# Regrouping the products with v and moving the row sums, transposes and cluster chain of a fused attention and expert kernel

## The chip, the cores and the metric

One core of a Trainium2 chip runs the whole program. The metric is device time in microseconds (us) for one execution, the median of several. Five engines work side by side and wait for each other by semaphores: PE (TensorE, matrix products), DVE (VectorE), ACT (ScalarE), POOL (GpSimd) and SP, which here issues DMAs. Each engine runs its instructions in the order in which they were written.

## The reference

Clustered attention for 4 batches of 8 heads, 768 tokens and head size 64, followed by a routed expert layer.

```python
def _attn_ref(q, k, v, centroids):
    ...
    q_assign = np.argmax(np.einsum('bhsd,hcd->bhsc', q_n, c_n), axis=-1)
    k_assign = np.argmax(np.einsum('bhsd,hcd->bhsc', k_n, c_n), axis=-1)
    mask = q_assign[:, :, :, None] == k_assign[:, :, None, :]
    scores = scale * np.matmul(q, k.transpose(0, 1, 3, 2))
    scores = np.where(mask, scores, -1000000000.0)
    scores = scores - np.max(scores, axis=-1, keepdims=True)
    attn = np.exp(scores)
    attn = attn / (np.sum(attn, axis=-1, keepdims=True) + 1e-09)
    return np.matmul(attn, v).astype(np.float32)
```

Then `_moe_ref` adds to each token whose `x @ w_skip` is positive the gated output of one of eight two-layer experts (512 to 1024 to 512), chosen by argmax.

## The kernel before

Two heads form a pair, and 16 pairs run one after the other (some 440 us); the experts follow (some 200 us) and are not touched. A pair has 24 steps, one per score tile: two query halves `hf` of 384 columns, six key tiles `kt` of 128, two heads `a`, so step s = 12 hf + 2 kt + a. `steps` fills a heap of tasks with times in units of one step, counted from the pair's step 0, and pops them in order of time: the tables PLAN, FIRST, GATES and SLOTS are these times. So they fix the order in which every engine's instructions are written; they are no times on the chip. A function that yields a number goes on that much later; one that yields a tuple goes on at that time of its own pair.

What recurs in each pair, with its lines:

- `score` (L631, L632): two products into one PSUM bank, exp by ACT into one of 12 PT buffers (L634), and a running sum over keys `acc` by POOL (L640, L646).
- `smax` (L582, L584), one per step, for the next pair: a product into a bank and a DVE maximum over it. `mneg` (L598), `mrows` (L606, L617) turn the maxima into rows of the next operands.
- `avs` (L657): the products of PT with v, two heads side by side in 64 columns each, accumulated over key tiles in bank 7. One call does GROUP = 3 key tiles, so there are four calls in a pair; ACT then moves the result to `oT`.
- `sims` (L488) and the chain `assign` / `first_max` (L521 to L528) on DVE give each token's cluster, two pairs ahead; `masks` (L545), `split_hi` (L429, ACT) and `split_lo` (L439, DVE) prepare operands.
- `sums` (L693), `recip` (L705, L710), `xout` (L756 transposes; L778 scaling by ACT, or L761 by DVE in the last three pairs) finish the pair before and store it.
- Once per batch (four pairs) the routing runs over three pairs: `logits_in`, then `route_gates` (L843, L847) with `choose` (L901 to L919) and `gate` (L928 to L945), then `route_c` (L955 to L981), `route_d` (L991 rhs, L996 product) and `route_e`.

PSUM has eight banks. `take` gives out seven of them first in, first out, and `give` puts one back; bank 7 belongs to `avs`. An engine that writes a bank again waits until the reader of its last contents is done.

Products of `score` and `smax` use the array as one block of 128 columns, `avs` as two of 64, `sims`, `sums` and `logits_in` as four of 32.

Of the kernel before, what the change touches and what calls it, by code (L numbers as in the profile page):

```python
# [13 lines left out]
F32 = mybir.dt.float32  # L14
# [4 lines left out]
AF = mybir.ActivationFunctionType  # L19
ALU = mybir.AluOpType  # L20
# [25 lines left out]


PLAN = {
    "load": -60.0, "load_v": -45.0, "weights": 72.0, "sims": -42.9, "assign": (-42.45, 0.07, 0.02, 2.0, 0.02, 0.02),
    "hi": (-40.35, -34.25), "masks": (-34.5, 0.12), "lo": (-34.35, -28.35), "copies": (-23.3, -23.2, -23.1),  # L50
    "smax": (-21.1, 1.0, -0.4), "mneg": (-9.0, 3.2), "mrows": ((-4.5, 0.2, 0.05), (5.5, 0.1, 0.05)),
    "av": 1.6, "oT": (3.5, 3.55), "sums": 29.2, "recip": 31.5, "xout": (31.52, 49.55, 37.55),
    "route": (29.25, 34.9, 58.9), "early": (85.4, 100.9),
}

GATES = (35.0, 35.4, 37.66, 43.67, 43.68, 49.66, 49.67, 49.68, 49.69, 49.7, 49.71, 50.5,
         53.16, 53.17, 53.18, 61.67, 61.68, 67.67, 67.68, 73.66, 73.67)
SLOTS = (59.1, 59.11, 59.12, 59.13, 73.7, 73.71, 77.16, 77.17, 77.18, 77.19, 79.66, 82.9, 83.1,
         91.67, 91.68, 97.66, 97.67, 97.68, 97.69, 97.7)
CODES = {91.67: 85.9, 91.68: 85.91}  # L60
FIRST = {
    0: {
        "load_v": -18.9, "sims": -20.0, "hi": (-19.9, -19.8, -19.7, -19.6), "assign": (-19.0, 0.1, 0.01, 0.01, 0.01, 0.01),
        "lo": (-18.7, -18.6, -16.9, -16.8), "masks": -17.0, "smax": (-14.0, 0.1, 14.1, 0.55), "mneg": (-12.85, 7.55),
        "mrows": ((-12.8, 0.1, 0.0), (8.2, 0.1, 0.0)),
    },
    1: {
        "sims": -42.2, "hi": (-42.4, -42.3), "lo": (-40.1, -40.0), "copies": (-20.9, -20.8, -20.7), "load_v": -14.0,
        "assign": (-36.83, 12.93, 0.2, 0.2, 0.2, 0.2), "masks": (-21.6, 0.1), "smax": (-16.3, 0.95, -0.1),
        "mneg": (-5.3, 5.9), "mrows": ((-4.3, 0.2, 0.05), (6.4, 0.1, 0.05)),  # L70
    },
    2: {
        "load": -62.0, "load_v": -37.0, "hi": (-34.25, -28.3), "lo": (-28.35, -22.35), "copies": (-23.3, -23.2, -22.2),
        "assign": (-34.6, 0.25, 0.02, 6.0, 0.02, 0.02), "masks": (-26.0, 0.12), "smax": (-17.6, 0.97, 0.0), "mneg": (-6.4, 5.2),
    },
    3: {"assign": (-41.95, 0.07, 0.02, 1.5, 0.02, 0.02)},
}

GROUP = 3


class Kernel:
# [242 lines left out]

    def tasks(self, i):

        p, last = {**PLAN, **FIRST.get(i, {})}, i == self.npair - 1
# [319 lines left out]
    def avs(self, i, hf, kts):  # L648
        c, nc = self.st[i], self.nc
        if kts[0] == 0:  # L650
            c["av"] = self.banks[7][:, :HALF + 1]
        av = c["av"]
        first = None
        for kt in kts:
# [9 lines left out]
        if kts[-1] == KT - 1:
            p = PLAN["oT"]
            if hf == 0:
                c["oT"] = self.OT[i % 5]
            last, oT = i == self.npair - 1, c["oT"][:, hf * HALF:(hf + 1) * HALF]
            if not last or hf == 0:
                yield 0.05 if last else 1.0  # L670
            vm = self.small.tile([P, 1], F32, name="vm")
            if last and hf == 0:
                nc.vector.tensor_copy(vm, av[:, HALF:])
                nc.vector.tensor_scalar(out=oT, in0=av[:, :HALF], scalar1=vm, scalar2=None, op0=ALU.add)
                return
            if not last and hf:
                nc.scalar.activation(out=vm, in_=av[:, HALF:], func=AF.Copy)
                yield p[hf] - 1.0
                nc.scalar.activation(out=oT, in_=av[:, :HALF], func=AF.Identity, bias=vm)
            else:  # L680
                if not last:
                    yield p[hf] - 1.0
                nc.scalar.activation(out=vm, in_=av[:, HALF:], func=AF.Copy)
                nc.scalar.activation(out=oT, in_=av[:, :HALF], func=AF.Identity, bias=vm)
# [459 lines left out]
    def ending(self, i):  # L1144
# [15 lines left out]
        for t, c, k in ((25.8, 0, 0), (25.87, 0, 1), (25.94, 0, 2), (25.95, 0, 3), (25.96, 1, 0), (26.05, 1, 1),  # L1160
# [363 lines left out]
```

## Time and profile before

| | us |
|---|---|
| median of 3 runs | 643.86 (643.77 to 643.98) |
| profiled execution, its own time | 643.63 |
| its span, first to last instruction | 641.9 |
| PE busy | 621.7 (97%) |
| DVE busy | 506.0 (79%) |
| ACT busy | 425.9 (66%) |
| POOL busy | 364.0 (57%) |

In the attention stage POOL's share is far above its mean: it is idle in the experts' stage. The granted clock of PE is the full one all the way (0.997 on average). A PE row's duration runs to the modelled end of a pipelined product; what a product costs PE is the step from its start to the next one's start.

### The profile page before, as it was taken

To read this page: it belongs to the slowest core of one execution; us is meant where nothing else is said; L and a number is where in the kernel's file an instruction comes from. 1 tells how busy PE (TensorE), PEld (TensorE's weight loads), DVE (VectorE), ACT (ScalarE), POOL (GpSimd) and SP (SyncE) were. 2 spreads that over 40 slices of the span, in tenths; PEclk is the share of its full clock that TensorE was granted. 3 is DMA by queue.
4 is the path that set the end of the run, shared out by engine and by line. 5 is a ranking of instruction groups with operands and counts; after the bars stand their busy time and mean duration, and the time that the engine had idled before them with its cause. 6 is when DMAs were issued, how large, how long until landed. Compare 5 with 4: busy or idle time off the path is not lost.

```text
span 641.9 us, 12202 instructions
## 1 busy us (share of the span) xinstructions
PE 621.7 (97%) x3873; PEld 459.2 (72%) x3873; DVE 506.0 (79%) x1047; ACT 425.9 (66%) x963; POOL 364.0 (57%) x384
## 2 busy tenths in 40 slices
PE   7899999999999999999999999999999999999994
PEld 3566776676667766666767676646799899899793
DVE  6898787699998869999879997885889765855721
ACT  7377788788778877877878878833644644645510
POOL 8697887867867967778777778522043212121101
PEclk9999999999999999999999999999999999999998
DMA  7397748866786466555754652332395766765610
GB/s 215 92 228 204 189 125 210 228 205 176 206 231 179 129 172 168 170 140 162 206 151 124 174 135 75 99 117 86 117 312 196 255 222 223 240 206 177 240 44 36
DMA packets 54322, 110.10 MB, mean 172 GB/s; under 512 B 8599, under 2 KB 22807, under 8 KB 54256
## 3 DMA queue, kind: packets, MB, share of 16 engines
q1 hardware_dynamic: 51232, 101.92, 54.7%
q0 software_dynamic: 2624, 7.18, 3.3%
q8 instruction: 32, 0.52, 0.3%
q14 instruction: 34, 0.28, 0.2%
q10 hardware_dynamic: 400, 0.20, 0.1%
HBM read 60.93 MB, written 10.55 MB: 111 GB/s over the span
## 4 chain that ended last, share of the span: by engine, by line
PE 72%; DMA 10%; issue 9%; DVE 7%; ACT 1%; POOL 0%; POOLq 0%; DVEq 0%; ACTq 0%
PE ps L657 20%; PE ps L631 11%; PE ps L582 11%; PE ps L632 10%; DMA out<-yo,idw 7%; DMA xg<-out,idr 2%; PE ps L488 2%; DVE M L584 2%; PE ph L1058 2%; PE ph L1057 2%; PE ph L1056 2%; PE ps L693 2%; PE ps L756 2%; PE py L1057 1%; PE py L1056 1%
## 5 line engine op out<-in xcount | busy, mean ns | idle before, releaser
L646 POOL TENSOR_TENSOR acc<-acc,PT 128x384 f32<-128x384 f32 x246 | 244.0, 1020 | 42.2 <-ACT PT L634 41.9
L634 ACT ACTIVATE PT<-ps 128x384 f32<-128x384 f32 x384 | 183.2, 492 | 74.2 <-PE ps L632 62.1
L584 DVE TENSOR_REDUCE M<-ps 128x1 f32<-128x384 f32 x384 | 198.5, 550 | 40.3 <-PE ps L582 40.0
L657 PE MATMUL ps<-PT,vt 128*64 128x385 f32 x768 | 138.4, 495 | 0.1
L631 PE MATMUL ps<-D 102*128 102x384 f32 x384 | 134.9, 351 | 2.3 <-DVE M L584 1.7
L582 PE MATMUL ps<-D 96*128 96x384 f32 x384 | 134.4, 356 | 1.0 <-ACT D L562 1.0
L632 PE MATMUL ps<-D 128*128 128x384 f32 x384 | 130.0, 339 | 0.0
L657 PEld LDWEIGHTS ps<-PT,vt 128*64 128x64 f32 x768 | 49.3, 136 | 59.9 <-issue 55.3
L631 PEld LDWEIGHTS ps<-D 102*128 102x128 f32 x384 | 72.8, 190 | 23.8 <-issue 18.6
L582 PEld LDWEIGHTS ps<-D 96*128 96x128 f32 x384 | 73.5, 192 | 21.0 <-issue 14.4
L640 POOL TENSOR_TENSOR acc<-PT 128x384 f32<-128x384 f32 x64 | 54.5, 870 | 58.4 <-ACT PT L634 37.1
L1214 POOL DMA_INDIRECT out<-yo,idw x15 | 20.0, 1335 | 112.6 <-DVE yo L1090 95.3
L632 PEld LDWEIGHTS ps<-D 128*128 128x128 f32 x384 | 73.0, 190 | 0.0
L1342 ACT ACTIVATE hh<-ph 128x256 fp32r<-128x256 f32 x56 | 21.4, 383 | 46.4 <-PE ph L1058 46.4
L1343 DVE SCALAR_TENSOR_TENSOR hl<-ph,hh 128x256 fp32r<-128x256 f32 x56 | 23.6, 422 | 33.6 <-ACT hh L1342 33.6
L1314 ACT ACTIVATE D<-wraw 128x1024 fp32r<-128x1024 f32 (+1 forms) x45 | 44.2, 1002 | 6.5 <-PE py L1058 4.7
L1056 PE MATMUL ph<-x2l,D 128*128 128x256 f32 x168 | 47.7, 284 | 0.0
L1057 PE MATMUL ph<-x2h,D 128*128 128x256 f32 x168 | 47.5, 283 | 0.0
L1056 PE MATMUL py<-D,hh 128*128 128x512 f32 x112 | 45.0, 402 | 0.0
L1315 DVE TENSOR_TENSOR D<-wraw,D 128x1024 fp32r<-128x1024 f32 (+1 forms) x29 | 34.3, 1183 | 6.3 <-ACT D L1314 5.6
L778 ACT ACTIVATE x<-ps,rs 128x64 f32<-128x64 f32 x162 | 36.1, 322 | 3.5 <-issue 1.2
L439 DVE TENSOR_TENSOR raw<-raw,D 128x768 fp32r<-128x768 f32 x28 | 38.2, 1363 | 0.0
(314 smaller groups left out, 1050.5 us busy)
## 6 DMA issues: line engine op xcount, KB each, us to landing
wraw<-w SPq DMA_DIRECT2D x72, 512.0 KB, 4.7
D<-D SPq DMA_DIRECT2D x124, 192.0 KB, 3.4
raw<-qk SPq DMA_DIRECT2D x16, 768.0 KB, 5.5
D<-raw SPq DMA_DIRECT2D x60, 192.0 KB, 4.2
vt<-v SPq DMA_DIRECT2D x16, 384.0 KB, 4.6
out<-x SPq DMA_DIRECT2D x31, 192.0 KB, 3.6
D<-mk SPq DMA_DIRECT2D x120, 24.0 KB, 2.0
out<-yo,idw POOLq DMA_INDIRECT x15, 4.3
```

Source lines behind the costliest of these rows:

```text
L439: eng.tensor_tensor(out=lo.bitcast(F32R), in0=lo, in1=c[f"hi{t}"].bitcast(F32), op=ALU.subtract)
L582: nc.tensor.matmul(sm, lhsT=c["qm"][a][0:96, j * P:(j + 1) * P], rhs=c["kb"][a][0:96, hf * HALF:(hf + 1) * HALF], start=True, stop=True)
L584: nc.vector.tensor_reduce(out=c["m"][:, j, a, hf:hf + 1], in_=sm, axis=AX.X, op=ALU.max)
L631: nc.tensor.matmul(ps, lhsT=c["kb"][a][:MR, ks], rhs=c["qm"][a][:MR, sl], start=True, stop=False)
L632: nc.tensor.matmul(ps, lhsT=c["kc"][a][:, ks], rhs=c["qc"][a][:, sl], start=False, stop=True)
L634: nc.scalar.activation(out=pt, in_=ps, func=AF.Exp, scale=D ** -0.5)
L640: nc.gpsimd.tensor_tensor(out=acc, in0=self.pt(i, s - 2)[:, :HALF], in1=pt, op=ALU.add)
L646: (nc.vector if dve else nc.gpsimd).tensor_tensor(out=acc, in0=acc, in1=pt, op=ALU.add)
L657: nc.tensor.matmul(av[a * D:(a + 1) * D, :], lhsT=c["vt"][:, kt, a * D:(a + 1) * D], rhs=self.pt(i, hf * 2 * KT + kt * 2 + a), start=(kt = ...
L1056: mm(ps, lhsT=ah, rhs=bl, start=first, stop=False)
L1057: mm(ps, lhsT=ah, rhs=bh, start=False, stop=False)
L1314: nc.scalar.activation(out=h[:, cs], in_=r[:, cs], func=AF.Copy)
```

## The change

A call of `avs` now takes four key tiles, and its tiles may lie in both query halves: three calls in a pair (two halves' key tiles 0 to 3; 4, 5 and 0, 1; 2 to 5). The last pair keeps groups of three. Each half has a bank of its own from the rotation, which now has eight banks, and `av_out` gives it back. `sums`, `recip`, the transposes of `xout`, and `mrows` stand next to a group of `avs`. `sims` and `sums` stand in front of different groups. `assign` is cut in two: the maximum, the comparison and the multiplication beside one group, the rest beside the next. Both `split_lo` of a pair, and most of the routing's DVE work, stand directly behind each other after a group. `xout` of the first half is scaled by DVE in every pair.

```diff
-    "av": 1.6, "oT": (3.5, 3.55), "sums": 29.2, "recip": 31.5, "xout": (31.52, 49.55, 37.55),
+    "av": 1.6, "oT": (0.35, 3.55), "sums": 33.06, "recip": 33.64, "xout": (33.66, 49.55, 41.55),
...
-GROUP = 3
+GROUP = (4, 3)
...
         self.free = deque(range(7))
+        self.spare = [7]
...
-            for g in range(0, KT, GROUP):
-                add(12 * hf + 2 * (g + GROUP) + p["av"], self.avs, hf, range(g, g + GROUP))
+        n = GROUP[last]
+        keys = [(hf, kt) for hf in range(2) for kt in range(KT)]
+        for g in range(n, 2 * KT + 1, n):
+            add(2 * g + p["av"], self.avs, keys[g - n:g])
...
-        b = self.held[key] = self.free.popleft()
+        b = self.held[key] = self.spare.pop() if key == ("av", 0) and self.spare else self.free.popleft()
...
+        mark, first = c["exp%d%d" % keys[-1]], True
+        for hf, kt in keys:
+            if kt == 0:
+                c["av", hf] = self.take(("av", hf), [P, HALF + 1])
+            av = c["av", hf]
             for a in range(2):
...
+            nc.scalar.activation(out=vm, in_=av[:, HALF:], func=AF.Copy)
...
+            nc.scalar.activation(out=oT, in_=av[:, :HALF], func=AF.Identity, bias=vm)
+            if last:
                 self.out_mark = self.newest()
+        self.give(("av", hf))
...
-        if i >= self.npair - 3:
+        if i >= self.npair - 3 or hf == 0:
             self.scale_out(i, hf, xp)
```

The first place is PE's order in a pair in the middle, around the products of `sims` (raw, cb) and `sums` (acc, ones); L582 and L586 are `smax`, L631/L632 and L635/L636 `score`, L606 and L610 `mrows`, L657 and L661 `avs`. Before:

```order
L488 MATMUL ps_85<-raw,cb_175 32x384 x2
L488 MATMUL ps_85<-raw,cb_179 32x384 x2
L693 MATMUL ps_82<-acc,ones 32x384 x4
L606 MATMUL ps_87<-ident,MX_190 128x128
L582 MATMUL ps_84<-D 128x384
```

Now, from the end of one stretch of scores:

```order
L492 MATMUL ps_81<-raw,cb_175 32x384 x2
L492 MATMUL ps_81<-raw,cb_179 32x384 x2
L586 MATMUL ps_88<-D 128x384
L764 MATMUL ps_83<-ident,oT_97 128x128 x3
L661 MATMUL ps_87<-PT,vt 64x385 x8
...
L701 MATMUL ps_82<-acc,ones 32x384 x4
L586 MATMUL ps_86<-D 128x384
L661 MATMUL ps_85<-PT,vt 64x385 x8
L610 MATMUL ps_84<-ident,MX_190 128x128
L713 MATMUL ps_88<-ident,sr 128x128 x3
L764 MATMUL ps_81<-ident,oT_98 128x128 x3
```

`sims` and `sums`, once one block, are two blocks before two groups of `avs`, and one `smax` product stands between each and its group.

The second place is DVE's order in a pair that runs `route_c` (rk, rank, hi, los) and the second half of `gate` (vals, g); raw is `split_lo`, M is `smax`. Before:

```order
L962 TENSOR_TENSOR rk<-ps_85,ohd 128x48
L966 TENSOR_REDUCE rank<-rk 128x6
L970 TENSOR_SCALAR hi<-rank 128x6
L973 SCALAR_TENSOR_TENSOR los<-hi,rank 128x6
L584 TENSOR_REDUCE M_199<-ps_83 128x1
L584 TENSOR_REDUCE M_199<-ps_86 128x1
L439 TENSOR_TENSOR raw<-raw,D 128x768
L942 CAST vals<-g 128x6
L945 TENSOR_TENSOR g<-g,vals 128x6
L584 TENSOR_REDUCE M_199<-ps_87 128x1
```

Now:

```order
L588 TENSOR_REDUCE M_199<-ps_87 128x1
L443 TENSOR_TENSOR raw<-raw,D 128x768 x2
L950 CAST vals<-g 128x6
L953 TENSOR_TENSOR g<-g,vals 128x6
L950 CAST vals<-g 128x6
L953 TENSOR_TENSOR g<-g,vals 128x6
L970 TENSOR_TENSOR rk<-ps_82,ohd 128x48
L974 TENSOR_REDUCE rank<-rk 128x6
L978 TENSOR_SCALAR hi<-rank 128x6
L981 SCALAR_TENSOR_TENSOR los<-hi,rank 128x6
L588 TENSOR_REDUCE M_199<-ps_81 128x1
```

Ten operations now stand between two `smax` maxima where at most four stood.

The third place is DVE's order at `route_d` (rhs), with the end of the cluster chain (mwc, oh, rows). Before:

```order
L710 RECIPROCAL rs<-ps_87 128x3x2 x2
L510 TENSOR_TENSOR eqc<-eqc,wts 128x384
L991 TENSOR_TENSOR rhs_2047<-rv,hs 128x30x8
L513 TENSOR_REDUCE mwc<-eqc 128x24
L515 TENSOR_TENSOR oh<-wts,mwc 128x384
L528 STREAM_TRANSPOSE rows<-oh 128x384
L584 TENSOR_REDUCE M_200<-ps_84 128x1
```

Now:

```order
L517 TENSOR_REDUCE mwc<-eqc 128x24
L519 TENSOR_TENSOR oh<-wts,mwc 128x384
L532 STREAM_TRANSPOSE rows<-oh 128x384
L999 TENSOR_TENSOR rhs_2088<-rv,hs 128x30x8 x2
L718 RECIPROCAL rs<-ps_83 128x3x2 x2
L769 TENSOR_TENSOR x<-ps_81,rs 128x384
L588 TENSOR_REDUCE M_200<-ps_84 128x1
```

Both rhs now come before the reciprocals, right behind the cluster chain, and the scaling of `xout`'s first half (x) follows them.

## Rows read from the trace of the kernel before

**Rows 1.** The page: busy time (share of span), and the chain that ended last.

```profile
PE 621.7 (97%) x3873; PEld 459.2 (72%) x3873; DVE 506.0 (79%) x1047; ACT 425.9 (66%) x963; POOL 364.0 (57%) x384
...
PE 72%; DMA 10%; issue 9%; DVE 7%; ACT 1%; POOL 0%; POOLq 0%; DVEq 0%; ACTq 0%
```

**Rows 2.** Timeline, PE: start, us, engine, line, op, out<-in, count [idle before <-releaser].

```profile
303.77 0.49 PE L657 MATMUL ps<-PT,vt 128*64 128x385 f32 x2
...
304.10 0.49 PE L657 MATMUL ps<-PT,vt 128*64 128x385 f32 x2
...
315.93 0.33 PE L632 MATMUL ps<-D 128*128 128x384 f32 x1
316.20 2.16 PE L657 MATMUL ps<-PT,vt 128*64 128x385 f32 x12
318.29 0.44 PE L582 MATMUL ps<-D 96*128 96x384 f32 x1
318.57 0.34 PE L631 MATMUL ps<-D 102*128 102x384 f32 x1
```

**Rows 3.** Timeline, PE: sims with sums in one block, and sums alone.

```profile
307.31 0.85 PE L488 MATMUL ps<-raw,cb 128*32 128x384 f32 x8
...
308.74 0.33 PE L606 MATMUL ps<-ident,MX 128*128 128x128 f32 x1
...
383.66 0.85 PE L693 MATMUL ps<-acc,ones 128*32 128x384 f32 x8
384.44 0.33 PE L606 MATMUL ps<-ident,MX 128*128 128x128 f32 x1
```

**Rows 4.** Timeline, PE, at route_d of the first batch.

```profile
185.76 0.33 PE L582 MATMUL ps<-D 96*128 96x384 f32 x1
187.13 0.38 PE L996 MATMUL ps<-rhs,oht 128*128 128x80 bf16 x6 [1.03 <-DVE M L584]
```

**Rows 5.** Timeline, PE and DVE: an smax product and its maximum, undisturbed.

```profile
248.60 0.34 PE L582 MATMUL ps<-D 96*128 96x384 f32 x1
...
248.98 0.56 DVE L584 TENSOR_REDUCE M<-ps 128x1 f32<-128x384 f32 x1 [0.16 <-PE ps L582]
```

**Rows 6.** Timeline, PE and DVE, first pair: PE waits for a maximum.

```profile
42.18 0.42 PE L582 MATMUL ps<-D 96*128 96x384 f32 x1
...
43.85 0.33 PE L582 MATMUL ps<-D 96*128 96x384 f32 x1
45.09 0.45 PE L631 MATMUL ps<-D 102*128 102x384 f32 x1 [0.90 <-DVE M L584]
...
44.51 1.91 DVE L584 TENSOR_REDUCE M<-ps 128x1 f32<-128x384 f32 x4
```

**Rows 7.** Timeline, POOL, beside rows 8.

```profile
268.72 1.68 POOL L640 TENSOR_TENSOR acc<-PT 128x384 f32<-128x384 f32 x2 [1.96 <-ACT PT L634]
270.36 7.92 POOL L646 TENSOR_TENSOR acc<-acc,PT 128x384 f32<-128x384 f32 x8
```

**Rows 8.** Timeline, DVE: split_lo and operations of the routing.

```profile
242.13 0.94 DVE L901 TENSOR_REDUCE L<-lp 128x54 f32<-128x432 f32 x1
...
265.09 0.73 DVE L973 SCALAR_TENSOR_TENSOR los<-hi,rank 128x6 f32<-128x6 f32 x1
...
266.67 0.94 DVE L439 TENSOR_TENSOR raw<-raw,D 128x768 fp32r<-128x768 f32 x1
267.54 0.17 DVE L942 CAST vals<-g 128x6 bf16<-128x6 f32 x1
267.75 0.17 DVE L945 TENSOR_TENSOR g<-g,vals 128x6 f32<-128x6 f32 x1
...
271.45 1.54 DVE L439 TENSOR_TENSOR raw<-raw,D 128x768 fp32r<-128x768 f32 x1
272.92 0.83 DVE L942 CAST vals<-g 128x6 bf16<-128x6 f32 x1
273.79 0.92 DVE L945 TENSOR_TENSOR g<-g,vals 128x6 f32<-128x6 f32 x1
```

**Rows 9.** Timeline, DVE, fourteenth pair: xout scaled by DVE.

```profile
386.96 0.56 DVE L761 TENSOR_TENSOR x<-ps,rs 128x384 f32<-128x384 f32 x1
```

More of the change, by code (lines that the diff above doesn't have):

```diff
@@ L48 @@
 PLAN = {
-    "load": -60.0, "load_v": -45.0, "weights": 72.0, "sims": -42.9, "assign": (-42.45, 0.07, 0.02, 2.0, 0.02, 0.02),
-    "hi": (-40.35, -34.25), "masks": (-34.5, 0.12), "lo": (-34.35, -28.35), "copies": (-23.3, -23.2, -23.1),
-    "smax": (-21.1, 1.0, -0.4), "mneg": (-9.0, 3.2), "mrows": ((-4.5, 0.2, 0.05), (5.5, 0.1, 0.05)),
-    "av": 1.6, "oT": (3.5, 3.55), "sums": 29.2, "recip": 31.5, "xout": (31.52, 49.55, 37.55),
-    "route": (29.25, 34.9, 58.9), "early": (85.4, 100.9),
-}
[L56 to L60, printed above, removed]
+    "load": -60.0, "load_v": -45.0, "weights": 72.0, "sims": -46.95, "assign": (-46.42, 0.02, 0.02, 0.02, (-38.41,), 0.02),
+    "hi": (-38.405, -38.40), "masks": (-32.5, 0.12), "lo": (-30.38, -30.37), "copies": (-22.1, -21.2, -21.1),
+    "smax": (-21.6, 1.0, -0.2), "mneg": (-9.2, 4.0), "mrows": ((-6.5, 0.2, 0.05), (9.62, 0.1, 0.05)),
+    "av": 1.6, "oT": (0.35, 3.55), "sums": 33.06, "recip": 33.64, "xout": (33.66, 49.55, 41.55),
+    "route": (33.45, 41.5, 65.5), "early": (85.4, 100.9),
+}
+GATES = (41.62, 41.63, 41.64, 41.65, 41.66, 49.66, 49.67, 49.68, 49.69, 49.7, 49.71, 50.5,
+         53.16, 53.17, 53.18, 65.67, 65.68, 65.69, 65.7, 73.66, 73.67)
+SLOTS = (65.71, 65.72, 65.73, 65.74, 73.7, 73.71, 73.72, 73.73, 73.74, 81.66, 81.67, 84.4, 84.6,
+         89.67, 89.68, 97.66, 97.67, 97.68, 97.69, 97.7)
+CODES = {89.67: 85.9, 89.68: 85.91}
 FIRST = {
@@ L63 @@
         "load_v": -18.9, "sims": -20.0, "hi": (-19.9, -19.8, -19.7, -19.6), "assign": (-19.0, 0.1, 0.01, 0.01, 0.01, 0.01),
-        "lo": (-18.7, -18.6, -16.9, -16.8), "masks": -17.0, "smax": (-14.0, 0.1, 14.1, 0.55), "mneg": (-12.85, 7.55),
-        "mrows": ((-12.8, 0.1, 0.0), (8.2, 0.1, 0.0)),
+        "lo": (-18.7, -18.6, -16.9, -16.8), "masks": -17.0, "smax": (-14.0, 0.1, 14.1, 0.7), "mneg": (-12.85, 9.3),
+        "mrows": ((-12.8, 0.1, 0.0), (9.65, 0.1, 0.0)),
     },
@@ L68 @@
         "sims": -42.2, "hi": (-42.4, -42.3), "lo": (-40.1, -40.0), "copies": (-20.9, -20.8, -20.7), "load_v": -14.0,
-        "assign": (-36.83, 12.93, 0.2, 0.2, 0.2, 0.2), "masks": (-21.6, 0.1), "smax": (-16.3, 0.95, -0.1),
-        "mneg": (-5.3, 5.9), "mrows": ((-4.3, 0.2, 0.05), (6.4, 0.1, 0.05)),
-    },
-    2: {
-        "load": -62.0, "load_v": -37.0, "hi": (-34.25, -28.3), "lo": (-28.35, -22.35), "copies": (-23.3, -23.2, -22.2),
-        "assign": (-34.6, 0.25, 0.02, 6.0, 0.02, 0.02), "masks": (-26.0, 0.12), "smax": (-17.6, 0.97, 0.0), "mneg": (-6.4, 5.2),
+        "assign": (-36.83, 12.93, 0.2, 0.2, 0.2, 0.2), "masks": (-21.6, 0.1), "smax": (-15.6, 0.95, -0.1),
+        "mneg": (-4.6, 6.6), "mrows": ((-3.8, 0.2, 0.05), (9.45, 0.1, 0.05)),
+    },
+    2: {
+        "load": -62.0, "load_v": -37.0, "sims": -38.9, "assign": (-38.42, 0.02, 0.02, 0.02, (-30.38,), 0.02), "hi": (-36.2, -30.3), "lo": (-22.39, -22.38), "masks": (-26.0, 0.12), "smax": (-17.6, 0.97, 0.0), "mneg": (-6.4, 5.2),
     },
-    3: {"assign": (-41.95, 0.07, 0.02, 1.5, 0.02, 0.02)},
 }
-GROUP = 3
+LAST = {"sums": 29.2, "recip": 31.5, "xout": (31.52, 49.55, 37.55)}
+END = {"mrows": ((-6.3, 0.2, 0.05), (5.5, 0.1, 0.05)), "mneg": (-9.2, 4.0)}
+GROUP = (4, 3)
 class Kernel:
@@ L326, in tasks @@
     def tasks(self, i):
-        p, last = {**PLAN, **FIRST.get(i, {})}, i == self.npair - 1
+        p, last = {**PLAN, **FIRST.get(i, {}), **({self.npair - 2: LAST, self.npair - 1: END}.get(i, {}))}, i == self.npair - 1
         r = [(s, lambda s=s: self.score(i, s)) for s in range(NS)]
@@ L646, in score, with avs @@
             (nc.vector if dve else nc.gpsimd).tensor_tensor(out=acc, in0=acc, in1=pt, op=ALU.add)
-    def avs(self, i, hf, kts):
+    def avs(self, i, keys):
         c, nc = self.st[i], self.nc
[L650 to L654, printed above, removed]
+        mark, first = c["exp%d%d" % keys[-1]], True
[3 more added lines that the diff above has]
+            av = c["av", hf]
             for a in range(2):
@@ L659, in avs @@
                                  skip_group_check=True)
-                if not first:
-                    first = self.newest()
-                    self.tc.add_manual_dep(first, c[f"exp{hf}{kts[-1]}"].name, mybir.DependencyInfo(
+                if first:
+                    first = False
+                    self.tc.add_manual_dep(self.newest(), mark.name, mybir.DependencyInfo(
                         mybir.DependencyClass.Sync, mybir.DependencyReason.DATA), reason="group")
[L664 to L675, printed above, removed]
-            if not last and hf:
[L677 to L684, printed above, removed]
@@ new lines, in avs, with av_out @@
+        for hf in range(2):
+            if (hf, KT - 1) in keys:
+                return self.av_out(i, hf)
+    def av_out(self, i, hf):
+        c, nc = self.st[i], self.nc
+        last, av = i == self.npair - 1, c["av", hf]
+        if hf == 0:
+            c["oT"] = self.OT[i % 5]
+        oT = c["oT"][:, hf * HALF:(hf + 1) * HALF]
+        if not last or hf == 0:
+            yield 0.05 if last else 0.3
+        vm = self.small.tile([P, 1], F32, name="vm")
+        if last and hf == 0:
+            nc.vector.tensor_copy(vm, av[:, HALF:])
+            nc.vector.tensor_scalar(out=oT, in0=av[:, :HALF], scalar1=vm, scalar2=None, op0=ALU.add)
+        else:
+            if not last and hf == 0:
+                yield PLAN["oT"][hf] - 0.3
+            nc.scalar.activation(out=vm, in_=av[:, HALF:], func=AF.Copy)
+            if not last and hf:
+                yield PLAN["oT"][hf] - 0.3
+            nc.scalar.activation(out=oT, in_=av[:, :HALF], func=AF.Identity, bias=vm)
+            if last:
```

2 lines of the change are left out of this document (1 added, 1 removed).

## Prediction

> **What bounds the kernel now.** I read the page first, then the list of PE's waits, then the timeline of PE with those of DVE and POOL beside it. PE is busy for 97% of the span and holds 72% of the chain that ended last [rows 1]. In the attention stage its products follow each other at a fixed step: a product of 384 columns comes 0.18 us after the one before, except where a block of another tiling begins or ends. PE waits for another engine in few places: at the start, and twice at `route_d`, where it stands for 1.03 us on DVE [rows 4]. So time can be won in two ways, by fewer PE steps and by fewer waits, and lost in one: DVE holding PSUM banks too long.
>
> **PE's own work.** A key tile of `avs` costs two steps of 0.33 us (304.10 less 303.77), so three cost 1.96. A whole group, from the last score product before it to the second product behind it, takes 318.57 - 315.93 = 2.64; less two ordinary steps of 0.18, that is 2.28 [rows 2]. A group's own overhead is therefore 2.28 - 1.96 = 0.32, made of a longer step before it (0.27 instead of 0.18), a longer one behind it (0.28 instead of 0.18) and slow first and last steps. There are 60 groups in the first 15 pairs and will be 45: 15 x 0.32 = **4.8 us less**.
>
> Against that, `sims` and `sums` part. Together they take 308.74 - 307.31 = 1.43; `sums` alone takes 384.44 - 383.66 = 0.78 [rows 3], and I take `sims` alone, with as many products, at the same. Two blocks are 1.56, which is 0.13 more, and the second block pays one more longer step before it (0.09) and one behind it (0.10) [rows 2]: 0.32 per pair. In 13 pairs both are there: 13 x 0.32 = **4.2 us more**. In the three pairs with `logits_in` these products no longer follow `sums` directly, and the block is entered once more: about 0.15 each, 0.4 in all. The sum of PE's own work is -4.8 + 4.2 + 0.4 = **-0.2 us**. The change takes out one block of 64 columns per pair and puts in one of 32: the array changes its tiling ten times in a pair before and after. What I don't see in the trace is a lone `smax` product between two tiled blocks. I charge it both longer steps; if one hides in the other, 13 x 0.1 = 1.3 us go. Bounds: -1.5 to +0.3.
>
> The Trainium skill, "TensorEngine Tiling (Array Packing)", section "Tiling Modes", says that a change of the tiling mode, though not of the tile alone, drains the engine. By that rule the ten changes that stay cost what they cost, and PE's sum would be zero; the longer steps of rows 2 agree with it.
>
> Transposes moved beside a group stay as they are: beside a group they stand already. One `smax`, score or transpose product more or less there is not.
>
> **The wait at route_d.** The product of `route_d` starts 187.13 - 185.76 = 1.37 after the one before, instead of 0.18 [rows 4]; it happens in two of three batches. The rhs are now made before the reciprocals and so before the three maxima that come ahead of this product. I take both waits as gone: 2 x 1.19 = **-2.4 us**; what is late next there is `xout`'s scaling, which no PE step waits for soon. Bounds: -2.4 to 0.
>
> **Piles on DVE.** This decides. An `smax` product's maximum normally ends 248.98 + 0.56 - 248.60 = 0.94 after the product's start [rows 5]. How late may it end? In the first pair the product of 42.18 had its maximum done at 44.51 + 0.55 = 45.06, and PE started the next score at 45.09 where 43.85 + 0.18 = 44.03 was due [rows 6]: with seven banks in turn, a maximum may end 1.85 after its product's start, and what is beyond that PE stands, one for one. So DVE may be 0.9 us behind.
>
> Some DVE operations wait for POOL. `split_lo` takes 0.94 with POOL idle (it was, for 1.96 us before 268.72) and 1.54 with POOL adding; a cast of six columns 0.17 or 0.83, a subtraction 0.17 or 0.92, each time until POOL's add had ended [rows 7, 8]. The Trainium skill, "SBUF — State Buffer", section "Who interferes with whom", says that VectorE and GpSimd share a pair of ports, that the one which issues first keeps it for the whole instruction and the other fully blocks. By it every such operation of a pile could wait for a whole add, which is the heavy rival below; rows 7 and 8 agree as far as they go.
>
> Now the window between the last `smax` product of a stretch and the first of the next, with a group of four tiles: 0.18, a transpose and the way into the group 0.24, the group 2.09 (318.29 - 316.20) + 2 x 0.33 = 2.75, and 0.28 + 0.18 behind it: 3.6 us; with the 0.9, and less the maximum itself (0.48 at its step in a run: 1.91 for four), DVE may do 4.0 us of other work there.
>
> In an ordinary pair it does two `split_lo`: 1.9 to 3.1. That fits, at no cost; without the window it would cost 3 us a pair. In the pair of `route_c` it does two `split_lo`, four operations of `gate` and four of `route_c` (0.6 for three small ones, and los 0.73) in one row, and some 0.2 more of window for `route_c`'s products. If POOL were idle all along: 1.9 + 4 x 0.17 + 0.6 + 0.2 = 3.4, nothing lost. If each waited as the rows with POOL busy: 3.1 + 2 x 0.83 + 2 x 0.92 + 1.3 = 7.9, 3.7 us lost. I take 3.1 for the two, since POOL still has adds of the stretch before; then two waiting and two free casts or subtractions (0.9 + 0.9 + 0.3), because its next adds need the scores behind the group; then 1.3: 6.5, or 2.3 over; less 0.3 for overlapping starts: **2.0 us** per batch. What is late next is the score product that needs the bank, and all of PE behind it.
>
> The same batch has three smaller piles. In `route_gates`' pair: two `split_lo`, two products of lp, the sum over heads (0.94) and one comparison that can wait: 0 to 1.0, taken 0.4. In `route_c`'s pair behind the next group, beside the first half of the cluster chain: two operations that can wait, 0 to 1.6, taken 0.2. In `route_d`'s pair one: 0 to 0.5, taken 0.1. Together 2.7 per batch, three batches: **+8.1 us**. Bounds 0 to 14: the upper one is 3 x 3.7 for the first pile and 3 for the rest, since a standing PE also starves POOL.
>
> **Edits at nothing.** The scaling of `xout`'s first half goes from ACT to DVE: 0.56 in each of 13 pairs [rows 9]. It stands where DVE would wait for the next products anyway, behind a group; without that cover it costs up to 7 us, and its bound is in the pile's. The bank of `avs` comes from the rotation, but ACT empties it before its turn. The two `split_hi` in one row, their DMAs, the loads and the masks' DMAs on SP have ten steps and more before a reader. POOL issues the early gather amid its adds; PE needs none of them soon. The first three pairs get other orders of the same work; one more or one less wait like that of rows 6 (1.06) is my bound, both ways.
>
> **The sum.** -0.2 - 2.4 + 8.1 = +5.5 on the profiled execution's own time of 643.63 us, so 649.1; the median of the runs shown stands 0.23 above that execution: **649.3 us**, slower by 0.8%.
>
> **Rivals.**
> *The piles fit.* POOL happens to be idle when DVE gets to them, or the phases fall well: 0 to 1 us instead of 8.1, and the rest stays: 643.86 - 0.2 - 2.4 = 641.3 to 642.2. For it: the pile of rows 8 (1.54 + 0.83 + 0.92 between two maxima) cost PE nothing. Against it: that pile was 3.3 long, the new one has three times as many operations. It decides at a pile of 4.2 us. Chance 0.25.
> *Fewer groups pay in full.* Parting `sims` from `sums` costs nothing, the lone product hides both switches, and the piles fit: 643.86 - 4.8 - 2.4 = 636.7. Rows 3 speak against it. Chance 0.05.
> *Half piles.* About 1 us per batch is lost: 643.86 - 2.6 + 3 = 644.3, no change. Chance 0.13.
> *Heavy piles.* POOL always gets the port first, or the first pairs add a wait: 643.86 - 2.6 + 14 = 655.3. Against it: with PE standing, POOL runs out of adds within four scores. Chance 0.12.
>
> **How the numbers follow.** The forecast has 0.45. Half piles lie within 0.2% of 643.86 (1.3 us, about what can be told from no change): same 0.13. The first two rivals are faster, 0.30; forecast and heavy piles slower, 0.57. The range leaves out the full pay and most of the heaviest piles: 640.3 (the piles fit, with 1 us won in PE's work or the first pairs) to 655.
>
> **What would show it.** Right: in the timeline of the pairs with `route_c` an idle stretch of PE of 1.5 to 2.5 us some 2 us behind a group, released by DVE's M; casts of 0.8 in the pile before it; ordinary pairs within 0.1 us of their 24.7; no wait before the product of rhs. Wrong: ordinary pairs shorter by 0.3 (the lone product hides a switch) or PE without waits in the routing pairs (the piles fit). A wait in every pair would mean that two `split_lo` with DVE's scaling overfill the window, which would cost more than I allow.

## The result, and the profile of the changed kernel

The changed kernel takes 650.43 us (median of 4 runs, 647.55 to 651.46) where the kernel before takes 643.82 (643.64 to 643.98): a ratio of 1.0097, 95% interval 1.0072 to 1.0121. It is slower by 1.0%; the prediction was 649.3, slower by 0.8%. The executions of the changed kernel lie 4 us apart, those of before 0.3. The profiled one took 649.98, its span is 648.3. One run of the kernel with one block, below, took 861.77 us at a granted clock of 0.654 and is left out of that kernel's median.

The page of the changed kernel, busy time and the chain that ended last, against [rows 1]:

```profile
PE 624.1 (96%) x3873; PEld 460.5 (71%) x3873; DVE 505.9 (78%) x1060; ACT 410.0 (63%) x885; POOL 365.9 (56%) x384
...
PE 67%; DMA 13%; issue 9%; DVE 8%; POOL 1%; ACT 1%; SPq 0%; POOLq 0%; DVEq 0%; ACTq 0%
```

PE holds 5 points less of the chain, DMA 3 and DVE 1 more. PE's waits, longest first (line, what it waited for, us in total, times, longest), of the changed kernel:

```profile
PE ps L492 <- DMA raw<-qk: 4.3, 2, 3.6
PE ps L635 <- DVE M L588: 3.8, 5, 1.1
```

Of before they were:

```profile
PE ps L996 <- DVE M L584: 2.1, 2, 1.0
PE ps L631 <- DVE M L584: 1.7, 2, 0.9
```

The two waits at `route_d` are gone, five waits of a score for a maximum are there, and one of `sims` for a load (3.57; the other of the two, 0.71, is at the start), which the prediction does not have. Where the 6.35 us between the two profiled executions went shows best by pair, from a pair's first score product to the next pair's (us; worked out from the starts of those products; pairs counted from the first; the right three columns are experiments, below):

| pairs | before | changed | no lone product | POOL idle | gate apart |
|---|---|---|---|---|---|
| first | 24.87 | 23.22 | 23.22 | 24.42 | 23.02 |
| second | 25.56 | 29.80 | 27.36 | 27.27 | 24.61 |
| ordinary (eighth) | 24.71 | 24.66 | 24.20 | 24.66 | 24.20 |
| with logits (fifth) | 26.65 | 26.74 | 26.20 | 26.74 | 26.20 |
| with `route_c` (sixth) | 24.97 | 26.43 | 26.04 | 24.81 | 24.46 |
| with `route_d` (seventh) | 26.19 | 25.45 | 25.05 | 25.45 | 24.56 |
| the last and what follows | 239.36 | 240.14 | 239.81 | 240.01 | 239.64 |

The ordinary pairs of a kernel agree with each other to 0.1, and so do its pairs with logits. Over the whole span, changed less before: first pair -1.65, second +4.24, the third, the ordinary ones and those with logits together +0.02, the three with `route_c` +4.39, the three with `route_d` -1.27, the last and what follows +0.78, and -0.17 before the first score. First and last belong together: the first pair now holds 8 of its 12 key tiles of `avs` where it held 9, and the last holds one more tile of its predecessor (0.65). Together they are -0.87.

**The second pair.** Timeline of PE, changed kernel (start, us, engine, line, op, out<-in, count, [idle before]):

```profile
44.63 0.33 PE L636 MATMUL ps<-D 128*128 128x384 f32 x1
48.53 1.51 PE L492 MATMUL ps<-raw,cb 128*32 128x384 f32 x8 [3.57 <-DMA raw<-qk]
49.97 0.69 PE L586 MATMUL ps<-D 96*128 96x384 f32 x1
50.59 3.43 PE L661 MATMUL ps<-PT,vt 128*64 128x385 f32 x16
53.95 0.44 PE L635 MATMUL ps<-D 102*128 102x384 f32 x1
```

PE stands for 3.57 on the load of `raw` for the fourth pair's `sims`. And what follows is slow: from `sims` to the next score 5.42, where an undisturbed block of `sims`, lone product and group take 0.78 + 0.37 + 2.74 = 3.89. The windows show why (busy times of the engines, then granted clock, DMA share, GB/s):

```profile
44.00:48.00 4.00, 0.96 (x6) 0.60 (x4) 1.10 (x2) 2.32 (x6) 3.72 (x5) 1.00 0.90 204
48.00:50.00 2.00, 1.47 (x9) 0.26 (x9) 0.00 (x0) 0.00 (x0) 0.00 (x0) 0.62 0.27 70
50.00:52.00 2.00, 2.00 (x10) 0.88 (x9) 1.27 (x3) 0.00 (x0) 0.00 (x0) 0.53 0.08 18
52.00:54.00 2.00, 2.00 (x15) 0.67 (x11) 2.00 (x4) 0.00 (x0) 0.00 (x0) 1.00 0.75 194
```

After the wait the granted clock is near 0.5, the lower level of 1.2 GHz, and full again from 52 on. Wait and slow products are 5.1; some 0.75 of it is given back by a wait that the second pair had before (a step of 0.93 instead of 0.18 at 53.0) and has no more.

SP's issues, changed kernel, and then before, say when that load went out:

```profile
38.00 1.14 SPq L436 DMA_DIRECT2D D<-D  x2
39.24 0.52 SPq L396 DMA_DIRECT2D raw<-qk  x1
39.81 1.36 SPq L436 DMA_DIRECT2D D<-D  x2
```

```profile
39.32 0.33 SPq L392 DMA_DIRECT2D raw<-qk  x1
39.70 2.99 SPq L432 DMA_DIRECT2D D<-D  x4
...
51.11 0.85 PE L488 MATMUL ps<-raw,cb 128*32 128x384 f32 x8
```

The load is issued at the same time in both. Before, it landed 6.7 later and had 5.1 to spare until its reader at 51.11. Now its reader is due at 44.9, 5.6 after the issue, and it lands 9.2 after it.

**The pile of route_c.** DVE and PE, sixth pair of the changed kernel, the place of [rows 8]:

```profile
169.24 2.63 DVE L443 TENSOR_TENSOR raw<-raw,D 128x768 fp32r<-128x768 f32 x2
...
171.79 0.83 DVE L950 CAST vals<-g 128x6 bf16<-128x6 f32 x1
...
172.66 0.17 DVE L953 TENSOR_TENSOR g<-g,vals 128x6 f32<-128x6 f32 x1
...
172.86 0.18 DVE L950 CAST vals<-g 128x6 bf16<-128x6 f32 x1
...
173.08 0.33 PE L636 MATMUL ps<-D 128*128 128x384 f32 x1
173.16 0.20 DVE L970 TENSOR_TENSOR rk<-ps,ohd 128x48 f32<-128x48 f32 x1
...
173.41 0.19 PEld L586 LDWEIGHTS ps<-D 96*128 96x128 f32 x1 [0.31 <-DVE rk L970]
...
174.04 0.91 DVE L981 SCALAR_TENSOR_TENSOR los<-hi,rank 128x6 f32<-128x6 f32 x1
174.05 0.33 PE L586 MATMUL ps<-D 96*128 96x384 f32 x1
...
174.88 3.33 DVE L588 TENSOR_REDUCE M<-ps 128x1 f32<-128x384 f32 x7
175.47 0.45 PE L635 MATMUL ps<-D 102*128 102x384 f32 x1 [1.09 <-DVE M L588]
```

From the first `split_lo` to the first maximum behind the pile DVE is away for 174.88 - 169.24 = 5.64. PE's step is 175.47 - 174.05 = 1.42 instead of 0.18: 1.24 lost. That is not the whole price. The `smax` product at 173.41 and its weight load (PEld) wait for rk, in the middle of the pile, which reads the bank of `route_c`'s products: a step of 0.33 instead of 0.18. Two more steps are 0.28. With POOL idle, where none of these four steps is longer, the pair takes 1.62 less (table). In the next pair, behind the end of `gate` and five operations of the routing, a step of 184.48 - 183.89 = 0.59 loses another 0.41; so it is in the eleventh pair, but not in the fifteenth.

In the fifteenth pair PE waits for ACT instead, which has not yet moved the result of `avs` out of its bank (`oT`):

```profile
406.21 0.45 PE L635 MATMUL ps<-D 102*128 102x384 f32 x1 [0.17 <-ACT oT L690]
```

It starts 0.51 after the product before it. That, and not a pile, is the 0.3 by which this pair is longer (24.95 against 24.66): with the second pile gone (the run with `route_c` one group earlier) it still takes 24.94.

**route_d**, against [rows 4]:

```profile
192.76 0.34 PE L586 MATMUL ps<-D 96*128 96x384 f32 x1
192.94 0.39 PE L1004 MATMUL ps<-rhs,oht 128*128 128x80 bf16 x6
```

The step before the product is 0.18, where it was 1.37.

### The profile page after: what moved, and what is told of

It reads as the page before. It is cut to its first block, busy times and chain, and to the rows that moved or that the text cites. A ratio compares the mean times of both kernels' runs of the same rounds, so it can differ in the third digit from the quotient of the medians.

```text
span 648.3 us, 12165 instructions
## 1 busy us (share of the span) xinstructions
PE 624.1 (96%) x3873; PEld 460.5 (71%) x3873; DVE 505.9 (78%) x1060; ACT 410.0 (63%) x885; POOL 365.9 (56%) x384
## 4 chain that ended last, share of the span: by engine, by line
PE 67%; DMA 13%; issue 9%; DVE 8%; POOL 1%; ACT 1%; SPq 0%; POOLq 0%; DVEq 0%; ACTq 0%
PE ps L661 17%; PE ps L635 10%; PE ps L586 9%; PE ps L636 9%; DMA out<-yo,idw 7%; DMA raw<-qk 3%; DVE M L588 2%; PE ps L492 2%; PE ps L701 2%; DMA xg<-out,idr 2%; PE ph L1066 2%; PE ph L1065 2%; PE ph L1064 2%; PE ps L764 1%; DVE raw L443 1%
## 5 line engine op out<-in xcount | busy, mean ns | idle before, releaser
L638 ACT ACTIVATE PT<-ps 128x384 f32<-128x384 f32 x384 | 180.1, 492 | 42.1 <-PE ps L636 31.2
L635 PE MATMUL ps<-D 102*128 102x384 f32 x384 | 136.9, 356 | 4.5 <-DVE M L588 3.8
L661 PE MATMUL ps<-PT,vt 128*64 128x385 f32 x768 | 135.7, 494 | 0.0
L586 PE MATMUL ps<-D 96*128 96x384 f32 x384 | 133.4, 355 | 1.0 <-ACT D L566 1.0
L636 PE MATMUL ps<-D 128*128 128x384 f32 x384 | 130.4, 340 | 0.0
L661 PEld LDWEIGHTS ps<-PT,vt 128*64 128x64 f32 x768 | 50.8, 136 | 63.0 <-issue 60.1
L635 PEld LDWEIGHTS ps<-D 102*128 102x128 f32 x384 | 73.2, 191 | 25.7 <-issue 7.2
L586 PEld LDWEIGHTS ps<-D 96*128 96x128 f32 x384 | 73.5, 192 | 22.1 <-ACT PT L638 8.7
L636 PEld LDWEIGHTS ps<-D 128*128 128x128 f32 x384 | 73.6, 192 | 0.0
L621 ACT ACTIVATE D<-ps,blocks 6x256 fp32r<-6x256 f32 x84 | 33.3, 457 | 16.1 <-PE ps L610 15.7
L443 DVE TENSOR_TENSOR raw<-raw,D 128x768 fp32r<-128x768 f32 x28 | 35.9, 1310 | 0.1
```

The source lines that it names most:

```text
L443: eng.tensor_tensor(out=lo.bitcast(F32R), in0=lo, in1=c[f"hi{t}"].bitcast(F32), op=ALU.subtract)
L586: nc.tensor.matmul(sm, lhsT=c["qm"][a][0:96, j * P:(j + 1) * P], rhs=c["kb"][a][0:96, hf * HALF:(hf + 1) * HALF], start=True, stop=True)
L635: nc.tensor.matmul(ps, lhsT=c["kb"][a][:MR, ks], rhs=c["qm"][a][:MR, sl], start=True, stop=False)
L636: nc.tensor.matmul(ps, lhsT=c["kc"][a][:, ks], rhs=c["qc"][a][:, sl], start=False, stop=True)
L638: nc.scalar.activation(out=pt, in_=ps, func=AF.Exp, scale=D ** -0.5)
```

## Experiments

Below, the profiled times of pairs are those of the table or are worked out in the same way. The diffs show only the entries that change; the rest of their lines is left out.

**The load in the second pair.** Only the fourth pair's entries change:

```diff
-    },
+    }, 3: {"sims": -42.9, "assign": (-41.95, 0.07, 0.02, 1.5, 0.02, 0.02)},
```

> The changed kernel, with only the sims and assign of the fourth pair put back four steps, to where they stood before. Theory A (the wait of 3.57 us for the load of raw, and the low granted clock behind it, which makes the next 28 products cost 1.4 us more, are the whole loss of the second pair): the second pair falls from 29.8 us to about 25, the time from 649.98 to 645.0, at most 646 if another wait of the second pair (the one of 0.9 us that the kernel before had there) comes back. Theory B (the DMA queue is behind as a whole, so the next reader of a transfer waits instead): the second pair stays above 28 and the time above 648. The runs of the changed kernel spread over 4 us; by A that spread is this wait and goes, by B it stays.

Measured: 647.48 (647.18 to 648.36), 3.0 below the changed kernel and above the 645 to 646 of theory A. The second pair falls from 29.80 to 25.82, `sims` starts at 50.65 without a wait, and the executions lie 1.2 apart instead of 4. So theory A holds for that pair. The profiled execution gained only 1.6, because in this execution the pile of `route_c` cost 1.8 more in the tenth pair and 0.6 in the pair behind it, with the granted clock down at 0.50 after two waits (0.73 for the bank that rk reads, 1.28 for a maximum): the pile's price varies too.

Is it the earlier reader or the later landing? The third pair's `split_hi` was put back, which on SP puts the load ahead of two transfers that had come before it:

```diff
-"hi": (-36.2, -30.3)
+"hi": (-34.25, -28.3)
```

> The changed kernel with the split_hi of the third pair back at its times of before. On SP this only puts the load of raw for the fourth pair ahead of all four transfers of split_hi instead of between them. It parts the wait in the second pair (2.5 to 4.1 us in the runs so far) into two causes. Theory A (the earlier sims are nearly all of it): the load lands 9 us after its issue as now, the wait stays at 3 us or more, the time at 649 to 650. Theory B (two transfers ahead of it on the same queue make the load land later, 8.6 to 9.7 instead of 6.7): it lands after about 7 us, the wait falls to 1.2 or less, PE's granted clock stays full behind it, and the time falls by 2.5 to 4, to 646 to 647.5.

Measured: 650.02 (649.41 to 651.82), no change. The load now goes out at 38.52, ahead of all four, and lands 10.0 after its issue, later still:

```profile
38.52 0.33 SPq L396 DMA_DIRECT2D raw<-qk  x1
38.90 4.93 SPq L436 DMA_DIRECT2D D<-D  x4
...
48.63 1.51 PE L492 MATMUL ps<-raw,cb 128*32 128x384 f32 x8 [2.95 <-DMA raw<-qk]
```

Theory B falls: the two transfers ahead of it are not why it lands late. In the profiles of all kernels with the new tables it took 7.9 to 10.0, with the DMA engines busy all the while (in the changed kernel a share of 0.85 to 1.10 from 38 to 48 us); what makes the difference to 6.7 was not found. With a landing at 6.7 the reader at 5.6 would have waited about 1.1; the rest of the wait is the later landing.

**The piles.** First, `route_c` and its four operations one group earlier, and the two of cum amid the scores:

```diff
-    "route": (33.45, 41.5, 65.5),
+    "route": (33.45, 41.5, 57.5),
-SLOTS = (65.71, 65.72, 65.73, 65.74, 73.7, 73.71, 73.72, 73.73, 73.74,
+SLOTS = (57.71, 57.72, 57.73, 57.74, 73.7, 73.71, 73.72, 77.2, 78.2,
```

> The changed kernel, with route_c and its four operations (rk, rank, hi, los) one group of avs earlier, behind the end of the cluster chain, and the two operations of cum amid the scores instead of behind the next group. Theory A (the pile on DVE is what PE waits for, one for one): the waits of 1.25 and 0.4 us go in all three batches, the pair of route_c falls from 26.43 to about 25.0, the time from 649.98 to 645.2. Rival (the pile only moves to the window of the reciprocals, or two split_lo with the four operations of gate overfill theirs alone): a wait of 0.5 us or more stands in the pair of route_c, and the time is 647 to 650.

Measured: 646.64 (645.74 to 647.60). The pairs with `route_c` fall from 26.43 to 25.51, those with `route_d` from 25.45 to 24.95: together 1.4 less per batch, where 1.65 was to go. The second wait is gone. Of the first, 0.55 of step is left, behind two `split_lo` and four operations of `gate` alone, 4.46 from the first to the first maximum:

```profile
170.69 2.62 DVE L443 TENSOR_TENSOR raw<-raw,D 128x768 fp32r<-128x768 f32 x2
...
173.24 0.83 DVE L950 CAST vals<-g 128x6 bf16<-128x6 f32 x1
...
174.52 0.71 DVE L953 TENSOR_TENSOR g<-g,vals 128x6 f32<-128x6 f32 x1
175.15 1.47 DVE L588 TENSOR_REDUCE M<-ps 128x1 f32<-128x384 f32 x3
...
175.75 0.44 PE L635 MATMUL ps<-D 102*128 102x384 f32 x1 [0.40 <-DVE M L588]
```

The piles, 5.64 and 4.46 long, cost 1.62 and 0.65 (0.55 and a step of 0.28 behind it): 1.2 less of pile gives back 1.0, nearly one for one. The window that the prediction put at 4.0, and at 4.2 with `route_c`'s products in it, lies at 3.8 by the shorter pile and at 4.0 by the longer one. In this execution the wait for the load was 4.07, which is why the time did not fall further.

Second, POOL:

```diff
-        elif kt > 1 and not (i == self.npair - 1 and hf and kt >= KT - 2):
+        elif kt > 1 and i == self.npair - 1 and not (i == self.npair - 1 and hf and kt >= KT - 2):
```

> The changed kernel, with POOL's running sums over keys left out except the first addition of each half and head (and the last pair's), so the row sums are incomplete; POOL is then idle for most of a pair. Theory A (the pile at route_c is made long by operations that wait for POOL): the two split_lo take 1.9 us instead of 2.6, the casts 0.17 instead of 0.83, los 0.73 instead of 0.91, in all 1.5 us less, and PE's wait of 1.25 us falls to 0 to 0.3, that of 0.4 to 0; the pair of route_c falls to 25.1 and the time by 3 to 4.5 us. Rival (the pile is too long by its number of operations, POOL matters little): the durations stay, the wait stays above 0.8 us, and the time falls by less than 1. The wait in the second pair stays in both.

Measured: 646.12 (644.22 to 647.21). The pairs with `route_c` come to 24.81, without a wait; in all three the pile fits. (The first pair is 1.2 longer than in the changed kernel; why was not looked into.) The same ten operations, with POOL idle:

```profile
168.40 1.81 DVE L443 TENSOR_TENSOR raw<-raw,D 128x768 fp32r<-128x768 f32 x2
170.14 0.17 DVE L950 CAST vals<-g 128x6 bf16<-128x6 f32 x1
...
171.31 0.17 DVE L978 TENSOR_SCALAR hi<-rank 128x6 f32<-128x6 f32 x1
171.51 0.17 DVE L981 SCALAR_TENSOR_TENSOR los<-hi,rank 128x6 f32<-128x6 f32 x1
171.74 3.74 DVE L588 TENSOR_REDUCE M<-ps 128x1 f32<-128x384 f32 x7
```

3.34 instead of 5.64: 2.3 us of the pile are waits for POOL's adds, and without them it is inside the window. The second, small wait stays at 0.41 in the first two batches; there the addition that was left in (the first of a half) runs beside the pile, so this run does not tell how much of that wait is POOL's. The Trainium skill, "SBUF — State Buffer", section "Who interferes with whom", says that of VectorE and GpSimd only one has the shared ports at a time. The trace agrees: a cast is 0.17 with POOL idle and up to 0.83 behind an add.

**The lone products.**

```diff
-    "sims": -46.95,
+    "sims": -46.43,
-    "sums": 33.06,
+    "sums": 33.57,
```

> The changed kernel, with the smax product that stands alone between sims and its group of avs, and the one between sums and its group, put ahead of sims and of sums: the blocks of 32 and of 64 columns then follow each other directly. Theory A (a lone product pays both longer steps, as I charged it, and a change from 32 to 64 columns costs no more than one of them): two longer steps of 0.1 fewer per block, so ordinary pairs fall from 24.66 to 24.3 or 24.4, 13 pairs, 3.5 to 5 us, the time 645 to 646.5. Rival (one switch hides in the lone product, or the direct change from 32 to 64 costs as much as two): ordinary pairs within 0.1 of 24.66, the time within 1.3 of 650. A second rival (the cluster chain and the reciprocals, now half a step later, push DVE's windows over): ordinary pairs above 24.8.

Measured: 642.07 (640.59 to 644.45), ratio to before 0.9975, interval 0.9958 to 0.9993: with two numbers changed the kernel is 8 us faster than the changed one, more than any of the theories has, and faster than before. Ordinary pairs fall by 0.46, those of the routing by about as much; 2.4 of the 8 are the second pair, where the wait for the load is 3.06 and the granted clock behind it stays full. PE at `sums`, changed kernel, and without the lone product:

```profile
314.84 0.85 PE L701 MATMUL ps<-acc,ones 128*32 128x384 f32 x8
315.62 0.44 PE L586 MATMUL ps<-D 96*128 96x384 f32 x1
315.99 2.81 PE L661 MATMUL ps<-PT,vt 128*64 128x385 f32 x16
318.73 0.33 PE L610 MATMUL ps<-ident,MX 128*128 128x128 f32 x1
```

```profile
308.63 0.85 PE L701 MATMUL ps<-acc,ones 128*32 128x384 f32 x8
309.41 2.81 PE L661 MATMUL ps<-PT,vt 128*64 128x385 f32 x16
312.15 0.33 PE L610 MATMUL ps<-ident,MX 128*128 128x128 f32 x1
```

The block of `sums` takes 0.78 and the group 2.74 in both; only the lone product's 0.37 leaves, and in a row of its kind that product takes 0.18. So it paid 0.19, both longer steps; nothing hid. At `sims` the three transposes of `xout` that stood behind the lone product now stand ahead of `sims` too, and that place gives the other 0.27; the two were not parted. A group of four takes the 2.74 that the prediction had (2.75). From 32 to 64 columns the array changes at no price beyond that.

**One block again.** On top of that, `sims` was joined with `sums`:

```diff
-"sims": -46.95, "assign": (-46.42, 0.02, 0.02, 0.02, (-38.41,), 0.02),
+"sims": -38.45, "assign": (-38.42, 0.02, 0.02, 0.02, (-30.38,), 0.02),
-"masks": (-32.5, 0.12), "lo": (-30.38, -30.37), "copies": (-22.1, -21.2, -21.1),
+"masks": (-28.0, 0.12), "lo": (-22.39, -22.38), "copies": (-22.1, -19.2, -19.1),
-"sums": 33.06,
+"sums": 33.57,
```

> The changed kernel with sims and sums in one block again, directly ahead of the second group, without a lone smax product; the first part of the cluster chain then stands in the window of the reciprocals, the rest in that of the third, and both split_lo in that of the first. Theory A (each change of the array's tiling costs about 0.23, as the lone products showed; a pair falls from 10 changes to 7, and one block of 16 products is 0.1 shorter than two of 8): ordinary pairs 24.66 - 0.69 - 0.1 = 23.9. Rival (the window of the reciprocals now holds 3.1 us of DVE work, that of split_lo 2.6 and the rest: one of them overfills): ordinary pairs 24.2 or more, with a wait of PE for a maximum in each. The routing pairs keep their piles or get worse; the fourth pair's sims come 8 steps later, so the wait in the second pair is gone. Time 637 to 642.

Measured: 648.84 (648.81 to 650.36), not 637 to 642; ratio to before 1.0074, interval 1.0054 to 1.0094. Ordinary pairs take 24.13, without waits: 0.07 less than with two blocks, not 0.3. My price of 0.23 for each change of the tiling is wrong. The Trainium skill, "TensorEngine Tiling (Array Packing)", section "Tiling Modes", has each change of the tiling mode drain the engine. Here, going from 10 changes in a pair to 8 gave 0.46 and from 8 to 7 gave 0.07, so a count of changes does not give the time. What costs, by these two runs, is a return to 128 columns between two blocks. The routing pairs got much worse (30.3 in the worst, with a wait of 2.65), since their piles now met other windows.

**Groups of four alone.** The kernel before with the new `avs` and its banks, and all tables as they were:

```diff
-GROUP = 3
+GROUP = (4, 3)
```

> The kernel before with one part of the change alone: groups of four key tiles, and the banks of avs from the rotation of eight. All the tables of times are those of before, so sims and sums stay one block amid the scores, the routing stays spread, ACT scales xout. Theory A (a group's own overhead is 0.32 and 15 go): ordinary pairs 24.71 - 0.32 = 24.4, the time 643.6 - 4.8 = 638.8; route_d's wait of 1.19 stays in two batches. Rival (two switches are what a group costs, at 0.23 each, and the transposes and other operations that stood in a row with a group no longer do): 24.25 to 24.4, 637 to 639. Rival (the longer groups hold PT buffers or banks too long, or DVE's operations amid the scores now miss the shelter of a group): new waits on ACT or on a maximum, pairs above 24.6, time above 642.

Measured: 691.26 (690.17 to 691.58), slower by 7.3%. The last theory holds, which has the mechanism but said no more of the size than "above 642". An ordinary pair takes 25.66 instead of 24.71. The eighth pair, DVE's work amid the scores:

```profile
215.56 1.19 DVE L444 TENSOR_TENSOR raw<-raw,D 128x768 fp32r<-128x768 f32 x1
...
216.67 1.00 DVE L1026 TENSOR_TENSOR cc<-ohd,ecode 128x48 f32<-128x48 bf16 x1
...
217.71 0.20 DVE L1029 TENSOR_REDUCE c<-cc 128x6 f32<-128x48 f32 x1
217.83 2.40 DVE L589 TENSOR_REDUCE M<-ps 128x1 f32<-128x384 f32 x5
...
218.44 0.44 PE L636 MATMUL ps<-D 102*128 102x384 f32 x1 [0.76 <-DVE M L589]
```

`split_lo` and two operations of the routing stand amid scores, with no group behind which DVE could catch up before PE needs a bank. There are 24 waits of a score for a maximum, 22.9 us, and behind the longest the granted clock is 0.50 for 6 us. The same groups and banks with the new tables take 650: without the new places behind the groups, groups of four cost far more than they save. Banks and group size were not tried apart.

**A better kernel.** Three mends together (no lone product, `route_c` one group earlier, the fourth pair's `sims` in the block of `sums`):

```diff
-    },
+    }, 3: {"sims": -38.45, "assign": (-38.42, 0.02, 0.02, 0.02, (-30.38,), 0.02),
+           "lo": (-22.39, -22.38), "copies": (-22.1, -19.2, -19.1), "masks": (-28.0, 0.12)},
```

> The changed kernel with three edits at once: no lone smax product beside sims and sums; route_c one group earlier and cum amid the scores; the fourth pair's sims in one block with sums beside the second group of the second pair, its cluster chain, split_lo and masks that much later. If the three add up: the changed kernel's 650.0, less 8 to 10 (ordinary pairs at 24.2, that is 13 x 0.46 = 6, and the places with logits), less 3 x 1.4 for the pile of route_c, less 4.0 for the wait in the second pair: 633 to 636, faster than the kernel before by 1.2 to 1.7%. Rival (the second pair's DVE work, now in the window of the reciprocals, makes a new wait; or what is left of the pile grows, since PE comes sooner to the next stretch): 637 to 640. The spread over executions should fall to under 1 us if the load of raw was its cause.

Measured: 636.48 (636.31 to 636.83), ratio 0.9883, interval 0.9867 to 0.9900. It is just past the upper end of what adding up gives: PE still waits for the pile of `gate`, 0.40 in two batches and 1.32 in the other, and the third pair takes 25.50 where it took 24.78 with the lone products gone alone. The executions lie 0.5 apart. Last, half of `gate`'s pile was taken apart:

```diff
-65.67, 65.68, 65.69, 65.7, 73.66, 73.67)
+65.67, 65.68, 69.2, 70.2, 73.66, 73.67)
```

> The kernel with the three mends, with the second two of the four operations of gate taken out of the pile behind the two split_lo and put singly amid the scores that follow. The wait that is left in the pairs of route_c is 0.40 us in two batches and 1.32 in the other. Theory A (the pile is still over the window by that much): the waits go, those pairs come to 24.7, and the time from 636.5 to 634.5 or 635.3. Rival (an operation of DVE amid the scores that waits for POOL's add costs as much there as in the pile): a wait of 0.3 to 1 us a few steps later, the time within 0.5 of 636.5 or above.

Measured: 634.21 (634.03 to 634.53), ratio 0.9848, interval 0.9834 to 0.9861: faster than the kernel before by 1.5%. All three pairs with `route_c` take 24.46, and PE waits for no maximum in them. Singly, those operations cost next to nothing.

## Why the prediction came out near, point by point

- **PE's own work, -0.2:** right. The third, the ordinary pairs and those with logits are +0.02 together. The lone product pays both longer steps, as charged, 0.19. That splitting costs about as much as 15 groups give is right for this order; in another order it need not cost that, as the edit of two numbers showed (-0.46 per pair). The gain of 15 groups by itself was not measured, since the run with the groups alone has other losses.
- **route_d's waits, -2.4:** right, both gone.
- **Piles, +8.1:** the place, the releaser and the windows were right, the term too large. The pairs with `route_c` lose 4.39 (4.86 against those with POOL idle, which are 0.16 shorter than before), where 6.0 was taken (2.0 per batch): its pile is 6.5 by my sum and 5.64 in the trace. Two `split_lo` took 2.6 and not 3.1, the four of `gate` 1.35 and not 2.1, with one waiting for POOL and not two; `route_c`'s four took 1.7 and not 1.3. The wait was to be 1.5 to 2.5 and is 1.09. The three smaller piles, taken at 2.1 in all, are 0.8: the one in the pair with logits (0.4) and the one taken at 0.1 are not there, and the second pile of `route_c`, taken at 0.2, is 0.41 in two batches of three. Together 5.2.
- **Edits at nothing:** here a step failed. "... the loads and the masks' DMAs on SP have ten steps and more before a reader" is false for the fourth pair's load of `raw`: its `sims` moved four steps earlier while the load did not. In the tables 13 steps are left between the two. On the chip SP, which sends one transfer right behind the other there, issues the load 5.6 us before `sims` is due, under six steps of some 1 us. The trace of before would have told it: 5.1 to spare, and the reader now 6.2 earlier (the four steps, and a first pair that is shorter). It cost 4.24 in the second pair, where I allowed one wait of 1.06 more or less. "The bank of `avs` comes from the rotation, but ACT empties it before its turn" fails too, once and at a small price: 0.3 in the fifteenth pair.
- **First and last pair:** -0.87, within that bound: the waits of [rows 6] went.

So -0.2 - 2.4 + 8.1 = +5.5 stood against 0.0 - 2.4 + 5.2 + 0.3 + 4.24 - 0.87 - 0.17 = +6.3. That the number is near is partly luck: a pile term 2.9 too large stood in for a load of 4.2 that I had not seen. The kernel is slower for two reasons, the load and the piles, of about equal weight, and only one was forecast. Neither rival with fitting piles came; the piles fit only with POOL idle or when taken apart.

## What to carry to other kernels

When a table of times moves a step earlier, go through every input of that step, loads included, and compare its time to spare in the trace, from the issue on the chip and not from the table, with the distance moved. Put narrow blocks of an array tiling directly beside each other, with no full-width product between them. A pile behind a long group is free up to the window that the banks allow, and an operation that can wait for another engine can take its longer duration there (here one of the four of `gate` and los did), so it is better placed alone amid the stream.

## What the runs showed of the hardware

- PE's waits cost more than their length when the granted clock falls behind them. After 3.57 and 4.07 us of waiting for the load, the products behind it ran at about half clock for some 4 us (1.5 us lost in the first case); after 3.06 and 2.48, in two other kernels, at full clock. After 2.65 in the kernel with one block it fell to 0.50 for some 6 us, and after 2.66 in the one with the groups alone too, so the length of a wait alone does not tell. After 2.95 with a wait of 0.6 just before it, and after two waits of 0.73 and 1.28 close together, it fell as well.
- One load of 768 KB took 6.7 to 10.0 us from issue to landing in the same place of the program, in kernels whose only differences were the order of a few other transfers and times. Being first on its queue did not help it.
